# Pooled attention and a max-out FFN on one core: a hand-written order of issue, token groups of 64, and big loads on ScalarE's queue

## The chip, the cores and the metric

The kernel runs on one core of a Trainium2 chip. The metric is the device time of one execution, in microseconds (us). Engines are named as in the profile: PE (TensorE's matmuls), PEld (its weight loads), DVE (VectorE), ACT (ScalarE), POOL (GpSimd), SP (SyncE). A q after a name (ACTq, SPq) is that engine issuing DMAs.

## The reference, cut to what matters

```python
# q, k, v: (8, 8, 576, 64) f32; w1..w3: (512, 768), w_out: (768, 512)
k_p = k.reshape(B, H, 72, 8, D).mean(axis=3)       # 576 keys -> 72
v_p = v.reshape(B, H, 72, 8, D).mean(axis=3)
attn = softmax(q @ k_p.T / 8)
x = (attn @ v_p), heads side by side               # (4608 tokens, 512)
h = maximum(maximum(x @ w1, x @ w2), x @ w3)       # (4608, 768)
out = h @ w_out                                    # (4608, 512) f32
```

## The kernel before

The work is two streams on one PE: eight batches of attention, and nine blocks of 512 tokens of the FFN. Block n can run once the batches that cover its tokens are done. The framework's scheduler interleaves them, and it chooses each engine's order. In names of tiles, `kt` and `vt` are loaded keys and values, `kp` and `vp` the same after the mean over 8 (a fold adds one half of a tile to the other), `xn` and `xT` the attention's result and its transpose, `pw` and `po` PE's results of the FFN's two stages, `osb` the output. These are the parts that the change touches (`...` marks cuts):

```python
NT, NR = 18, 32                      # 18 groups of 32 tokens
def load(b, after=None):
    kt = ld.tile([96, 6, POOL, D], F32, ...)              # two buffers in turn
    vt = ld.tile([Sp, H, POOL, D], F32, ...)
    ... loads = [nc.sync.dma_start(out=kt, in_=ksrc)]     # SyncE's queue
    loads.append(nc.sync.dma_start(out=vt, in_=vsrc))
    ...
def prep(b, kt, vt, qb):             # the mean over 8: three folds
    if b < 2:  fold(nc.vector, kt ...)                    # k of batches 0 and 1 on DVE
    else:      fold(nc.gpsimd, kt ...)                    # the others on POOL
    fold(nc.gpsimd, vt, ...)                              # v always on POOL
...
def moe(n):                          # one block
    ...                              # 72 matmuls into pw, ACT cast, two DVE maxima
    for mm in range(4):
        ...                          # 6 matmuls into po
        osb = sb3.tile([128, C], F32, ...)                # three buffers in turn
        nc.scalar.copy(out=osb, in_=po)
        for u in range(4):                                # four stores of 64 KB
            nc.sync.dma_start(out=dst[:, g, :], in_=osb[32 * u:32 * u + 32, :])
```

The softmax here doesn't subtract the row's maximum and nothing guards it: scores larger than these inputs give would overflow.

Of the kernel before, what the change touches and what calls it, by code (L numbers as in the profile page):

```python
# [14 lines left out]
def kernel(  # L15
# [24 lines left out]
    NT = 18  # L40
    NR = 32
    NI = NT // 2
# [10 lines left out]
    etp = ctx.enter_context(tc.tile_pool(name="etp", bufs=16))  # L53
    psp = ctx.enter_context(tc.tile_pool(name="psp", bufs=1, space=PSUM))

    def load(b, after=None):
        kt = ld.tile([96, 6, POOL, D], F32, name="kt", tag="kt")
        ksrc = k[b].rearrange("h s d -> (h s d)").rearrange(
            "(p i j d) -> p i j d", p=96, i=6, j=POOL)
        vt = ld.tile([Sp, H, POOL, D], F32, name="vt", tag="vt")  # L60
        vsrc = v[b].rearrange("h (sp j) d -> sp h j d", j=POOL)
        if b == 0:
            loads = [nc.sync.dma_start(out=kt[:, i:i + 3], in_=ksrc[:, i:i + 3])
                     for i in (0, 3)]
        else:
            loads = [nc.sync.dma_start(out=kt, in_=ksrc)]
        loads.append(nc.sync.dma_start(out=vt, in_=vsrc))
        qb = ld.tile([128, 2, NT, D], BF16, name="qb", tag="qb")
        nc.gpsimd.dma_start(out=qb, in_=q[b].rearrange(
            "h s d -> (h s d)").rearrange("(g p t d) -> p g t d", g=2, p=128, t=NT))  # L70
        if after is not None:
            for x in loads:
                tc.add_manual_dep(x.ins, after.ins.name, mybir.DependencyInfo(
                    mybir.DependencyClass.Sync, mybir.DependencyReason.DATA),
                    reason="weights first")
        return kt, vt, qb

    first = load(0)

    ident = const.tile([128, 128], BF16, name="ident", tag="ident")  # L80
    make_identity(nc, ident)
    identh = const.tile([128, 128], F16, name="identh", tag="identh")
    make_identity(nc, identh)

    w_sb = [const.tile([128, KCH, DFF], F16, name=f"mw{wi}", tag=f"mw{wi}")
            for wi in range(3)]
    wo_sb = const.tile([128, JCH, C], F16, name="mwo", tag="mwo")
    w_dma = [nc.gpsimd.dma_start(out=t,  # L88
                                 in_=wap.rearrange("(kc p) j -> p kc j", p=128))
             for t, wap in zip(w_sb, (moe_w1, moe_w2, moe_w3))]  # L90
    nc.gpsimd.dma_start(out=wo_sb,
                        in_=moe_w_out.rearrange("(jc p) c -> p jc c", p=128))

    vp_all = const.tile([Sp, B, H, 65], F16, name="vp", tag="vp")
    nc.vector.memset(vp_all, float(POOL))

    kz_all = [const.tile([128, 2, H, Sp], BF16, name=f"kz{i}", tag=f"kz{i}")
              for i in range(2)]
    for kz in kz_all:
        nc.vector.memset(kz, 0.0)  # L100

    xT = const.tile([128, KCH, TOK], F16, name="xT", tag="xT")

    def prep(b, kt, vt, qb):
        kp2 = sb2.tile([96, 6, 2, D], BF16, name="kp2", tag="kp2")
        def fold(e, t, outs):
            for n in (4, 2):
                e.tensor_tensor(out=t[:, :, 0:n, :], in0=t[:, :, 0:n, :],  # L108
                                in1=t[:, :, n:2 * n, :], op=ALU.add)
            for o in outs:  # L110
                e.tensor_tensor(out=o, in0=t[:, :, 0, :], in1=t[:, :, 1, :],  # L111
                                op=ALU.add)

        if b < 2:
            for i in (slice(0, 3), slice(3, 6)):
                fold(nc.vector, kt[:, i], [kp2[:, i, 0, :], kp2[:, i, 1, :]])
        else:
            fold(nc.gpsimd, kt, [kp2[:, :, 0, :], kp2[:, :, 1, :]])
        fold(nc.gpsimd, vt, [vp_all[:, b, :, 0:D]])

        qT = sb2.tile([128, 2, NI, 128], BF16, name="qT", tag="qT")
        qTf = qT.rearrange("p g i c -> p (g i) c")
        for m in range(3):
            pqt = psp.tile([128, 6, 128], BF16, name="pqt", tag="tr", bufs=1)
            for u in range(6):
                n = 6 * m + u
                g, i = n // NI, n % NI
                nc.tensor.transpose(pqt[:, u, :], qb[:, g, 2 * i:2 * i + 2, :],  # L128
                                    ident)
            if b == 0 and m == 1:  # L130
                nc.vector.tensor_copy(out=qTf[:, 6 * m:6 * m + 6, :], in_=pqt)
            else:
                nc.scalar.copy(out=qTf[:, 6 * m:6 * m + 6, :], in_=pqt)  # L133

        pkt = psp.tile([128, 6, 96], BF16, name="pkt", tag="tr", bufs=1)
        for i in range(6):
            nc.tensor.transpose(pkt[:, i, :], kp2[:, i, :, :], ident[0:96, 0:96])  # L137
        kz = kz_all[b % 2]
        for par in range(2):
            rows = slice(64 * par, 64 * par + 64)  # L140
            nc.vector.tensor_copy(
                out=kz[rows, par].rearrange("p h (r i) -> p h r i", i=6),
                in_=pkt[rows].rearrange("p i (h r) -> p h r i", h=H))
        return qT, kz

    def heads(b, qT, kz):
        ets = []
        for h in range(H):
            psc = psp.tile([Sp, 2, 512], F32, name="psc", tag="att", bufs=2)
            mov = qT[:, h // 4, :, 32 * (h % 4):32 * (h % 4) + 32]  # L150
            for par in range(2):
                nc.tensor.matmul(psc[:, par, 0:288], kz[:, par, h, :], mov,  # L152
                                 start=True, stop=True)
            et = etp.tile([Sp, S], F16, name="et", tag="et")
            nc.scalar.activation(  # L155
                out=et.rearrange("p (i a r) -> p i a r", a=2, r=NR),
                in_=psc[:, :, 0:288].rearrange("p a (i r) -> p i a r", r=NR),
                func=FT.Exp, scale=1.0 / 64.0)
            ets.append(et)
        return ets  # L160

    def values(b, ets):
        for c0, keep in ((0, 0), (128, 0), (256, 0), (384, 0), (448, 64)):
            pav = psp.tile([128, 2, 512], F32, name="pav", tag="att", bufs=2)
            for h in range(H):
                nc.tensor.matmul(  # L166
                    pav[:, h // 4, 65 * (h % 4):65 * (h % 4) + 65],
                    ets[h][:, c0:c0 + 128], vp_all[:, b, h, :],
                    start=True, stop=True)
            pv = pav[:, :, 0:260].rearrange("p g (h e) -> p g h e", e=65)  # L170
            rcp = sb3.tile([128, 2, 4], F32, name="rcp", tag="rcp")
            nc.vector.reciprocal(out=rcp, in_=pv[:, :, :, 64])
            xn = sb3.tile([128, 2, 4, D], F16, name="xn", tag="xn")
            nc.vector.tensor_tensor(  # L174
                out=xn, in0=pv[:, :, :, 0:D],
                in1=rcp.to_broadcast([128, 2, 4, D]), op=ALU.mult)
            pxt = psp.tile([128, KCH, 128], F16, name="pxt", tag="tr", bufs=1)
            for kc in range(KCH):
                nc.tensor.transpose(  # L179
                    pxt[:, kc, :],  # L180
                    xn[:, kc // 2, 2 * (kc % 2):2 * (kc % 2) + 2, :], identh)
            g0 = S * b + c0
            nc.scalar.copy(out=xT[:, :, g0 + keep:g0 + 128],  # L183
                           in_=pxt[:, :, keep:128])

    def moe(n):
        col = slice(NB * n, NB * n + NB)
        hT = sb2.tile([128, JCH, NB], F16, name="hT", tag="hT")
        for jc in range(JCH):
            t = None  # L190
            for wi in range(3):
                pw = psp.tile([128, NB], F32, name=f"pw{wi}", tag="pw", bufs=3)
                for kc in range(KCH):
                    nc.tensor.matmul(pw, w_sb[wi][:, kc, bass.ts(jc, 128)],  # L194
                                     xT[:, kc, col],
                                     start=(kc == 0), stop=(kc == KCH - 1))
                if wi == 0:
                    t = sb3.tile([128, NB], F16, name="t0", tag="t0")
                    nc.scalar.copy(out=t, in_=pw)  # L199
                elif wi == 1:  # L200
                    t1 = sb3.tile([128, NB], F16, name="t1", tag="t1")
                    nc.vector.tensor_tensor(out=t1, in0=t, in1=pw, op=ALU.max)  # L202
                    t = t1
                else:
                    nc.vector.tensor_tensor(out=hT[:, jc, :], in0=t, in1=pw,  # L205
                                            op=ALU.max)
# [23 lines left out]
    while done < TOK // NB:  # L230
        moe(done)
        done += 1
# [30 lines left out]
```

## Time and profile before

| | before |
|---|---|
| time, median of the first 4 runs | 289.27 us (289.17 to 290.36) |
| span of the profiled run | 288.2 us |
| first FFN matmul (`pw`) | 43.97 us |
| period of a block with one batch of attention | 27.3 to 27.7 us |
| last matmul to end of span | 6.9 us |

The first part of the page gives each engine's busy time, its share of the span and its instructions; the `PEclk` row of the slices gives the clock that PE was granted, in tenths:

```profile
PE 248.6 (86%) x1664; PEld 131.2 (46%) x1664; DVE 129.3 (45%) x224; ACT 128.0 (44%) x218; POOL 117.4 (41%) x68
PEclk9999999999999999999999999999999999999996
```

Only PE is near full. The clock's row shows full from the start, but the trace has no clock record before 48.1 us, and the prediction found matmuls of half speed in the head, so this row says nothing before the first record. The prediction shows the rest of the reading: a head of 44 us, a full body and a tail.

### The profile page before, as it was taken

How to read it: one execution, taken by the hardware profiler on the slowest of the kernel's cores; microseconds unless marked ns; L12 is line 12 of the kernel's file. 1: busy time of each engine (PE TensorE's matmuls, PEld its weight loads, DVE VectorE, ACT ScalarE, POOL GpSimd, SP SyncE). 2: the span in 40 equal slices, each digit the busy share in tenths (PEclk: the TensorE clock that was granted, in tenths of full speed). 3: DMA queues.
4: the chain of work that ended last, by engine and by line, in shares of the span. 5: the costliest groups of instructions: out<-in, count | busy, mean ns of one | idle time of the engine just before them, and what ended most of it. 6: DMA issues, size and time to landing. Idle time of an engine off the chain costs nothing.

```text
span 288.2 us, 4331 instructions
## 1 busy us (share of the span) xinstructions
PE 248.6 (86%) x1664; PEld 131.2 (46%) x1664; DVE 129.3 (45%) x224; ACT 128.0 (44%) x218; POOL 117.4 (41%) x68
## 2 busy tenths in 40 slices
PE   0254049999999999999999999999999999999990
PEld 0132044564545455545554565456455544444440
DVE  7420083483238334724571557057505832533520
ACT  1134024753575267535753663565357533222230
POOL 6048006999999999999282300000000000000000
PEclk9999999999999999999999999999999999999996
DMA  7999999898839959975912700320040005014013
GB/s 189 255 228 199 261 239 229 190 219 234 193 111 216 202 141 214 235 174 119 206 31 72 141 20 0 98 50 0 2 123 23 2 9 138 1 27 120 3 45 102
DMA packets 17190, 36.47 MB, mean 127 GB/s; under 512 B 2736, under 2 KB 5040, under 8 KB 16496
## 3 DMA queue, kind: packets, MB, share of 16 engines
q1 hardware_dynamic: 12624, 28.32, 38.6%
q0 software_dynamic: 4544, 7.87, 15.3%
q8 instruction: 13, 0.21, 0.3%
q14 instruction: 9, 0.07, 0.1%
HBM read 34.60 MB, written 9.44 MB: 153 GB/s over the span
## 4 chain that ended last, share of the span: by engine, by line
PE 77%; DMA 14%; ACT 2%; DVE 1%; issue 1%; POOL 1%; SPq 0%; ACTq 0%; POOLq 0%
PE pw L194 47%; PE po L211 15%; DMA mw<-in_moe_w_dram 7%; PE psc L152 6%; PE pxt L179 4%; DMA out_dram<-osb 4%; DMA kt<-in_k_dram 3%; PE pav L166 3%; PE pqt L128 3%; ACT xT L183 2%; PE pkt L137 1%; DVE kt L108 1%; POOL mw L88 1%; ACT osb L215 0%; DVE xn L174 0%
## 5 line engine op out<-in xcount | busy, mean ns | idle before, releaser
L194 PE MATMUL pw<-xT,mw 128*128 128x512 f16 x648 | 163.8, 382 | 0.7 <-ACT xT L183 0.7
L194 PEld LDWEIGHTS <-mw 128*128 128x128 f16 x648 | 60.4, 98 | 51.0 <-issue 1.1
L202 DVE TENSOR_TENSOR t<-t,pw 128x512 f16<-128x512 f16 x54 | 37.1, 687 | 100.0 <-PE pw L194 97.6
L108 POOL TENSOR_TENSOR vt<-vt 72x2048 f32<-72x2048 f32 (+1 forms) x16 | 54.8, 3427 | 36.3 <-DMA vt<-in_v_dram 35.7
L199 ACT CAST t<-pw 128x512 f16<-128x512 f32 x54 | 31.6, 585 | 48.2 <-PE pw L194 47.7
L211 PE MATMUL po<-mwo,hT 128*128 128x512 f16 x216 | 48.1, 379 | 0.0
L205 DVE TENSOR_TENSOR hT<-t,pw 128x512 f16<-128x512 f16 x54 | 37.1, 686 | 16.5 <-PE pw L194 13.8
L155 ACT ACTIVATE et<-psc 72x576 f16<-72x576 f32 x64 | 37.4, 645 | 11.4 <-PE psc L152 11.3
L215 ACT COPY osb<-po 128x512 f32<-128x512 f32 x36 | 21.1, 587 | 36.2 <-PE po L211 34.7
L183 ACT COPY xT<-pxt 128x512 f16<-128x512 f16 (+1 forms) x40 | 21.8, 544 | 33.5 <-PE pxt L179 33.3
L211 PEld LDWEIGHTS <-hT 128*128 128x128 f16 x216 | 21.1, 98 | 25.5 <-DVE hT L205 1.7
L108 POOL TENSOR_TENSOR kt<-kt 96x1536 f32<-96x1536 f32 (+1 forms) x12 | 31.4, 2617 | 0.4
L152 PE MATMUL psc<-qT,kz 128*72 128x288 bf16 x128 | 27.9, 304 | 2.4 <-ACT et L155 1.5
L133 ACT COPY qT<-pqt 128x768 bf16<-128x768 bf16 x23 | 18.4, 801 | 24.0 <-PE pqt L128 23.7
L174 DVE TENSOR_TENSOR xn<-pav,rcp 128x512 f16<-128x512 f32 x40 | 26.7, 684 | 0.4
L179 PE MATMUL pxt<-identh,xn 128*128 128x128 f16 x160 | 16.5, 229 | 11.4 <-DVE xn L174 10.8
L128 PE MATMUL pqt<-ident,qb 128*128 128x128 bf16 x144 | 13.2, 234 | 13.7 <-DMA qb<-in_q_dram 12.0
L152 PEld LDWEIGHTS <-kz 128*72 128x72 bf16 x128 | 14.0, 117 | 19.5 <-issue 8.8
L179 PEld LDWEIGHTS <-xn 128*128 128x128 f16 x160 | 11.9, 102 | 21.9 <-DVE xn L174 17.4
L166 PE MATMUL pav<-vp,et 72*128 72x65 f16 x320 | 18.8, 200 | 3.3 <-POOL vp L111 3.3
L128 PEld LDWEIGHTS <-qb 128*128 128x128 bf16 x144 | 10.9, 105 | 20.5 <-DMA qb<-in_q_dram 12.0
L166 PEld LDWEIGHTS <-et 72*128 72x128 f16 x320 | 15.6, 103 | 7.3 <-ACT et L155 3.2
(23 smaller groups left out, 72.9 us busy)
## 6 DMA issues: line engine op xcount, KB each, us to landing
vt<-in_v_dram SPq DMA_DIRECT2D x8, 1152.0 KB
out_dram<-osb SPq DMA_DIRECT2D x144, 64.0 KB, 1.7
kt<-in_k_dram SPq DMA_DIRECT2D x7, 1152.0 KB, 10.4
qb<-in_q_dram POOLq DMA_DIRECT2D x8, 576.0 KB, 12.1
mw<-in_moe_w_dram POOLq DMA_DIRECT2D x3, 768.0 KB, 18.3
kt<-in_k_dram SPq DMA_DIRECT2D x2, 576.0 KB, 6.8
mwo<-in_moe_w_out_dram POOLq DMA_DIRECT2D x1, 768.0 KB, 25.4
```

Of the source, the lines that this page charges most:

```text
L108: e.tensor_tensor(out=t[:, :, 0:n, :], in0=t[:, :, 0:n, :], in1=t[:, :, n:2 * n, :], op=ALU.add)
L128: nc.tensor.transpose(pqt[:, u, :], qb[:, g, 2 * i:2 * i + 2, :], ident)
L152: nc.tensor.matmul(psc[:, par, 0:288], kz[:, par, h, :], mov, start=True, stop=True)
L155: nc.scalar.activation(out=et.rearrange("p (i a r) -> p i a r", a=2, r=NR), in_=psc[:, :, 0:288].rearrange("p a (i r) -> p i a r", r=NR), ...
L166: nc.tensor.matmul(pav[:, h // 4, 65 * (h % 4):65 * (h % 4) + 65], ets[h][:, c0:c0 + 128], vp_all[:, b, h, :], start=True, stop=True)
L179: nc.tensor.transpose(pxt[:, kc, :], xn[:, kc // 2, 2 * (kc % 2):2 * (kc % 2) + 2, :], identh)
L183: nc.scalar.copy(out=xT[:, :, g0 + keep:g0 + 128], in_=pxt[:, :, keep:128])
L194: nc.tensor.matmul(pw, w_sb[wi][:, kc, bass.ts(jc, 128)], xT[:, kc, col], start=(kc == 0), stop=(kc == KCH - 1))
L199: nc.scalar.copy(out=t, in_=pw)
L202: nc.vector.tensor_tensor(out=t1, in0=t, in1=pw, op=ALU.max)
L205: nc.vector.tensor_tensor(out=hT[:, jc, :], in0=t, in1=pw, op=ALU.max)
L211: nc.tensor.matmul(po, hT[:, jc, bass.ts(mm, 128)], wo_sb[:, jc, :], start=(jc == 0), stop=(jc == JCH - 1))
```

## The change

Its intent is to start the FFN earlier and to keep PE covered. Every engine now issues exactly in written order. Groups are of 64 tokens, so that a tile of 128 tokens has two stores of 128 KB. Batches 0 and 1 are partly loaded as 16-bit and pooled on PE. The first exps take four heads at once. Weights come in column thirds. Blocks 0 and 1 start in halves. The loads of k and v of batches 2 to 7 go from SyncE's to ScalarE's queue. The core of the diff, cut:

```diff
-    NT = 18
-    NR = 32
+    NG = 9
+    NR = 64
...
+    ctx.enter_context(tc.manual_schedule())
...
+    def load_kv(b, name, src, eng, dtype, parts):
+        t = ld.tile([Sp, H, POOL, D], dtype, name=name, tag=name[:2])
...
+    hT0 = new_hT()
+    side = queries(1)
+    loads_on = nc.scalar
+    def load(b):
+        kts[b], x = load_kv(b, "kt", k, loads_on, F32, 1)
+        vts[b], y = load_kv(b, "vt", v, loads_on, F32, 1)
+        if b == 2:
+            after(x + y, last_early[0])      # wait for v of batch 1
+        load_q(b)
+    for slot, _ in enumerate(hidden(0, hT0)):      # block 0, first part
+        ...
+    for slot, _ in enumerate(project(0, hT0)):     # block 0, second part
+        ...
+    load(2)
+    load(3)
+    fold_k(2, nc.gpsimd)
+    fold_v(2)
+    ...
+    for n in range(1, TOK // NB):                  # blocks 1 to 8
+        if n + 2 < B:
+            fold_k(n + 2, nc.gpsimd); fold_v(n + 2)
+        if n + 3 < B:
+            load(n + 3)
+        nxt = batch(n + 1) ...                     # one step of it per slot
-            for u in range(4):
+            for u in range(2):
```

## The prediction

> **What bounds the kernel now.** I read first the slices of the page: which engine is full, and from when.
>
> ```profile
> PE   0254049999999999999999999999999999999990
> DVE  7420083483238334724571557057505832533520
> ACT  1134024753575267535753663565357533222230
> ```
>
> One slice is 7.2 us. TensorE (PE) is nearly idle for six slices and full to the last; no other engine is full. So there are three spans: a head (to 44 us), a body bound by PE, and a tail. The chain that ended last, in order of time (start, length, what), says what the head waits for:
>
> ```profile
> 4.47 21.32 DMA mw<-in_moe_w_dram
> 25.81 9.92 DMA kt<-in_k_dram
> 35.75 1.82 DVE kt L108 x2
> 37.88 0.66 DVE xn L174
> ...
> 43.97 0.59 PE pw L194
> ...
> 239.83 15.54 PE pw L194 x72
> 255.37 5.18 PE po L211 x24
> ```
>
> The weights land at 25.8. Then batch 1's keys are fetched, and VectorE (DVE), which takes its instructions in order, stands before their fold while batch 0's `xn`, whose input has been ready since about 28, waits behind it. The waits name it (total, times, longest, in us):
>
> ```profile
> DVE kt L108 <- DMA kt<-in_k_dram: 17.4, 2, 16.7
> PE pxt L179 <- DVE xn L174: 10.8, 2, 10.0
> ```
>
> So the head loses 16.7 us to an order. For the body I read stretches (length, busy PE, PEld, DVE, ACT, POOL, clock, DMA share, GB/s):
>
> ```profile
> 157.40:184.80 27.40, 27.29 (x198) 14.61 (x196) 13.54 (x24) 15.12 (x26) 2.68 (x3) 1.00 0.29 61
> 239.80:260.50 20.70, 20.70 (x98) 9.40 (x96) 8.25 (x12) 5.76 (x10) 0.00 (x0) 1.00 0.20 51
> 281.30:288.20 6.90, 0.00 (x0) 0.00 (x0) 0.00 (x0) 0.59 (x1) 0.00 (x0) 0.67 0.39 102
> ```
>
> A block of the FFN alone takes 20.72 us (15.54 + 5.18 of the chain: 96 matmuls of 216 ns); with one batch of attention in it 27.49 (the period of the `po` groups in the chain), so a batch costs 6.77. From 44.0 to 281.3 there are nine blocks and seven batches: 186.5 + 47.4 = 233.9 of the 237.3; the other 3.4 went where stores stood behind loads on SyncE's queue (70 to 84). The tail is 6.9.
>
> **What the Trainium skill says.** (1) "Perfetto Trace Analysis", DMA Instruction — HWDGE: the semaphore wait of such a DMA is held by the issuing sequencer, which goes on to its next instruction only after the descriptors are made. Here the trace agrees for SyncE: its queue waited 16.6 us for POOL to free `vt` buffers, and stores stood behind. The change gives these loads to ScalarE (ACT), which also has all the evacuations. (2) "DMA: Bandwidth & Descriptors", Issuing engines are not separate DMA queues: another issuer brings no bandwidth; no run shows this yet. (3) "TensorE: Matmul & The Clock Gate", Part 1: an idle PE falls to half clock and takes some 3.4 us of work to return. The trace agrees: four score matmuls of 288 columns took 1.18 us in the head, about 240 ns each from start to start, against about 125 in the body. (4) "ScalarE: Activation LUTs", What ACT_TABLE_LOAD costs: 186 ns + 0.833 ns a column; that gives 666 for 576 columns, the trace has 645.
>
> **The change, part by part.**
>
> *Head.* Removed: the wait of 16.7. Batch 0 is hand-ordered, q before v, weights in column thirds. DMA: q, v (16-bit) and k of batch 0 are 0.6 + 0.6 + 1.2 MB as written; at the 250 GB/s of 7 to 19 us in this trace they land near 11.5, the first third of the weights (0.8 MB at 200 GB/s) near 16. The chain on the engines: half a k near 6.0; its fold on DVE 1.2 + 0.7 + 2 x 0.4 = 2.7 (from 0.936, 0.546 and 0.339 us of the 768, 384 and 192 column folds); transpose and copy 1.1; second fold 2.7; a copy of q 0.5: scores start near 13.2. ACT then has two exps of 1024 columns (1.04 each by the skill's formula) and four of 640 (0.72), with waits for the second half of k and q: last exp near 20.8 (old total 8 x 0.645, so the merging itself saves under 0.5). First values, `xn` twice, transposes, copies (0.3, 0.9, 0.9, 0.3, 0.6): the FFN starts near S = **23.5** instead of 44. The new pooling of v on PE (16 x 0.11) fits between the exps.
>
> *Block 0.* 20.7 of FFN and 0.1 for halves; the rest of batch 0's outputs 1.3; batch 1: pooling k on PE 8 x 0.216 = 1.7, v 1.7, transposes 1.3, scores 2.0. Together 28.9, with 1.0 of small stalls 29.9; the last copy to `osb` ends 0.8 later: T = 23.5 + 30.7 = **54.2**.
>
> *The loads of batches 2 and 3.* They are written after this block, and an engine issues in written order: ACT issues k2 and v2 at T, although the DMA engines have been free since about 40. In the old trace one such load alone runs at
>
> ```profile
> DMA packets 642, 1.57 MB, mean 192 GB/s; under 512 B 43, under 2 KB 43, under 8 KB 608
> ```
>
> (stretch 69.8 to 78), so 1.18 MB takes 6.1 + 2 = 8.1 us. Then POOL folds. POOL, start and length:
>
> ```profile
> 61.51 6.95 POOL L108 TENSOR_TENSOR vt<-vt 72x2048 f32<-72x2048 f32 x2
> 68.53 1.27 POOL L111 TENSOR_TENSOR vp<-vt 72x512 f16<-72x512 f32 x1
> ```
>
> A fold of v is 8.2, a fold of k (two outputs) 9.5. So k2 is folded at T + 17.6 and v2 at T + 25.8. Two things wait for that. Block 1's second slot transposes k2: PE stands until T + 17.6. Worse, load(4) is written before block 1, and its tiles are the third in two buffers: its v may start only when v2 is folded, and ACT waits for that **before** block 1's first cast. So block 1 resumes near T + 25.8 + 0.6 (wait, issue) + 1.0 (cast, copy) = T + 27.4 = **81.6**. Before the stall PE does five steps of batch 1's outputs and two half units, to about T + 5.0: some **22 us** of idle PE.
>
> *Body after it.* Eight blocks 165.8, less 0.9 done; rest of batch 1: 0.7; six batches. Scores now take three matmuls (320 + 192 + 64 columns, about 0.255 a head, 2.0 as before, because the padded keys give full-width weight loads); transposes 1.0 + 0.3 + 1.1, values 1.35: 5.8, plus 0.5 for stalls (before 1.0; one step per slot should halve them) = 6.3 each, 37.8. End of block 1 without cover 1.0; half clock after the stall 1.7. Sum 206.1: last matmul at 287.7. Later loads should not block: POOL needs 17.7 a batch against 27 a block.
>
> *Tail.* Two stores instead of four: 8 instructions at about 0.45 instead of 16, so about 2 less: 4.9. Span 292.6, plus 1.1 (289.3 against a span of 288.2): **293.7, say 294**.
>
> In one line: head −20.5, store stalls −3.4, attention −2.8, tail −2.0, against pooling and batch 0's outputs +4.8, bare stretches at both block ends, cold clock and small stalls some +6, the new stall +22.
>
> **Rivals.** *No stall*: if k2 and v2 came early, the 22 and the 1.7 fall away: about 270, 7% faster. For it: the diff makes load(2) wait for batch 1's v, which has a point only if it could be issued earlier, and nobody moves 20 us of head to lose it again. Against it: everything on ACT is in written order, and batch 1's v is pooled before. *Only PE's wait on k2*: if ACT did not block, PE resumes near T + 18 and then waits a little for v2: about 285. For it: a queue that holds waits apart from the engine; against it, the skill and SyncE's waits. *DMA-bound*: weight thirds have runs of 512 bytes written; were they twice as slow, k1 and the output weights would come about 8 us late and block 0 end later: 298 to 302. For it: DMA share near 1 until 44; against it, at 200 GB/s everything for block 0 lands by 37, while the output weights are wanted at about 45.
>
> **Range and chances.** The stalled course, chance 0.8, centres on 294 with some 5 us either way (S by 2, folds and landing by 3, batches by 3), so 2% above 289.3 (295.1) lies inside it: slower 0.34, same 0.43, faster 0.03. The other 0.2 is mostly faster (0.17). Range 272 to 302.
>
> **What would show it.** PE's slices: full from the fourth or fifth, then two to four empty slices near 58 to 82, then full. In the waits, ACT's queue (the load of v) for POOL's fold of v, above 15 us; PE for a transpose of k. Block period near 27.0, last stretch 20.7, tail near 5. It is wrong if the first `pw` comes after 30, if k2 is issued before 45, if ACT works on while its load waits, or if a period exceeds 28.

## The result

| | before | after |
|---|---|---|
| time, median | 289.27 us | 299.12 us (298.32 to 300.39, 4 runs) |
| first FFN matmul | 43.97 | 23.60 |
| end of block 0 | 74.0 | 54.5 |
| end of block 1 | 102.4 | 114.7 |
| last matmul | 281.3 | 292.9 |
| tail | 6.9 | 4.6 |

The changed kernel is 3.4% slower: the ratio is 1.0336, with a 95% interval of 1.0291 to 1.038. A ratio here is the mean time of one kernel's runs over that of the other's of the same rounds, so it is not quite the ratio of the medians. Executions over 1.5% slower than the fastest of the same kernel are left out of the means. The result is correct.

The changed kernel leads by 19.5 us after block 0 and trails by 12.3 us after block 1. The whole story lies in block 1, which takes 60.2 us instead of 28.3. The slices of the page after (7.4 us each) show the hole:

```profile
PE   7498999430079999999999999999999999999993
POOL 8451000039999998399249918950000000000000
PEclk9689999955557999999999999999999999999999
```

PE works from the first slice on, runs near full, and then there is a hole of four slices (4, 3, 0, 0). POOL is idle before the hole (four slices of 0) and becomes full in it. The clock is at half (5) for four slices. The waits (engine, line, releaser; total, times, longest) name who stood:

```profile
ACT t L265 <- POOL vp L121: 17.7, 1, 17.7
PE pkt L157 <- ACT xT L204: 16.0, 2, 15.8
ACT xT L204 <- DMA out_dram<-osb: 7.7, 1, 7.7
```

The chain that ended last, in order of time, follows the hole (start, length, what):

```profile
57.44 6.80 issue
64.24 4.51 POOL kt L118
...
80.65 1.27 POOL vp L121
82.72 0.50 ACT xT L204
83.26 0.64 PE pkt L157 x8
```

And the timeline of ACT shows how it came about. A line is start, length, engine, what; in brackets, how long it had idled and what ended that:

```profile
54.69 0.61 ACTq L70 DMA_DIRECT2D kt<-in_k_dram  x1
55.39 0.31 ACTq L70 DMA_DIRECT2D vt<-in_v_dram  x1
55.80 1.01 ACTq L70 DMA_DIRECT2D kt<-in_k_dram  x1
56.85 5.94 ACTq L70 DMA_DIRECT2D vt<-in_v_dram  x1
...
81.94 0.31 ACTq L70 DMA_DIRECT2D vt<-in_v_dram  x1
82.35 0.37 ACT L265 CAST t<-pw 128x256 f16<-128x256 f32 x1 [17.67 <-POOL vp L121]
```

The first four are k and v of batches 2 and 3, issued at the end of block 0. The last is batch 4's v. It goes out only when POOL has folded v of batch 2 (80.65 + 1.27 = 81.92), and the cast behind it, whose input was ready, waits 17.67 us. From 54.5 to 83.2 PE works 4.5 us of 28.7. Outside block 1 the change does what it was meant to: 20.4 us off the head, 2.3 us off the tail, and blocks of 27.2 to 27.6.

### The profile page after: what moved, and what is told of

Read it like the earlier page. It is cut to its first block, busy times and chain, and to the rows that moved or that the text cites. A ratio compares the mean times of both kernels' runs of the same rounds, so it can differ in the third digit from the quotient of the medians.

```text
span 297.5 us, 4634 instructions
## 1 busy us (share of the span) xinstructions
PE 258.7 (87%) x1853; PEld 143.3 (48%) x1853; DVE 126.2 (42%) x230; ACT 132.3 (44%) x224; POOL 123.2 (41%) x73
## 4 chain that ended last, share of the span: by engine, by line
PE 78%; POOL 6%; DVE 5%; DMA 4%; issue 4%; ACT 2%; SPq 0%; ACTq 0%; DVEq 0%; POOLq 0%
PE pw L260 45%; PE po L290 14%; PE psc L180 6%; PE pqt L150 4%; PE pav L209 3%; DMA kt<-in_k_dram 3%; PE pxt L200 3%; POOL kt L118 2%; POOL vt L118 2%; DVE kz L160 2%; DMA out_dram<-osb 1%; PE pvp L139 1%; PE pkt L157 1%; DVE xn L217 1%; ACT xT L204 1%
## 5 line engine op out<-in xcount | busy, mean ns | idle before, releaser
L260 PE MATMUL pw<-xT,mw 128*128 128x512 f16 (+1 forms) x696 | 164.0, 370 | 1.6 <-ACT xT L204 1.3
L268 DVE TENSOR_TENSOR t<-t,pw 128x512 f16<-128x512 f16 (+1 forms) x58 | 37.7, 651 | 81.2 <-PE pw L260 42.3
L265 ACT CAST t<-pw 128x512 f16<-128x512 f32 (+1 forms) x58 | 32.3, 557 | 56.7 <-PE pw L260 36.0
L118 POOL TENSOR_TENSOR kt<-kt 72x2048 f32<-72x2048 f32 (+1 forms) x12 | 41.1, 3426 | 32.1 <-issue 21.1
L185 ACT ACTIVATE et<-psc 72x576 f16<-72x576 f32 (+2 forms) x62 | 40.7, 662 | 15.8 <-PE psc L180 15.7
L271 DVE TENSOR_TENSOR hT<-t,pw 128x512 f16<-128x512 f16 (+1 forms) x58 | 37.7, 649 | 15.6 <-PE pw L260 13.7
L118 POOL TENSOR_TENSOR vt<-vt 72x2048 f32<-72x2048 f32 (+1 forms) x12 | 41.1, 3427 | 0.5
L217 DVE TENSOR_TENSOR xn<-pav,rcp 128x512 f16<-128x512 f32 x40 | 27.6, 691 | 1.4
L180 PE MATMUL psc<-qT,kz 128*128 128x64 bf16 (+3 forms) x192 | 26.7, 253 | 1.1 <-DVE qT L152 0.7
L180 PEld LDWEIGHTS <-kz 128*128 128x128 bf16 x192 | 18.8, 100 | 16.1 <-issue 1.9
L152 ACT COPY qT<-pqt 128x768 bf16<-128x768 bf16 (+2 forms) x23 | 18.1, 785 | 17.7 <-PE pqt L150 17.7
```

Source lines behind the costliest of these rows:

```text
L118: e.tensor_tensor(out=t[:, :, 0:n, :], in0=t[:, :, 0:n, :], in1=t[:, :, n:2 * n, :], op=ALU.add)
L180: nc.tensor.matmul(out, kz_all[b % 2][:, f % 2, h, :], qTs[b][:, n + i0:n + i1, 64 * (h % 2):64 * (h % 2) + 64], start=True, stop=True)
L185: nc.scalar.activation(out=out, in_=in_, func=FT.Exp, scale=1.0 / 64.0)
L217: nc.vector.tensor_tensor(out=xn, in0=pv[:, :, :, 0:D], in1=rcp.to_broadcast([128, 2, 4, D]), op=ALU.mult)
L260: nc.tensor.matmul(pw, w_sb[wi][:, kc, bass.ts(jc, 128)], xT[:, kc, col], start=(kc == 0), stop=(kc == KCH - 1))
L265: nc.scalar.copy(out=t, in_=pw)
```

## The experiments

There were twelve runs, all correct; the kernel before ran beside each (medians 288.96 to 289.48). Block 1 takes 60.2 us in the changed kernel. In each run I read three things: the length of block 1, the length of block 2, and the time.

| run | block 1 | block 2 | time (median) | ratio to before, 95% |
|---|---|---|---|---|
| changed kernel | 60.2 | 27.2 | 299.12 | 1.029 to 1.038 |
| e1_loads_sync | 51.2 | 31.4 | 294.44 | 1.013 to 1.022 |
| e6_load4_late | 50.9 | 36.2 | 298.64 | 1.028 to 1.037 |
| e6b_load4_mid | 50.8 | 30.9 | 292.94 | 1.009 to 1.015 |
| e2_early_sync | 40.6 | 27.2 | 279.59 | 0.961 to 0.971 |
| e8_spaced_loads | 50.8 | 30.1 | 292.00 | 1.003 to 1.013 |
| e9_fixed_slots | 39.4 | 30.9 | 281.68 | 0.970 to 0.977 |
| e9b_more_osb | 37.6 | 28.2 | 277.21 | 0.953 to 0.961 |
| e10_slots_only | 60.4 | 27.2 | 299.37 | 1.030 to 1.042 |
| e3_warm_stall | 60.1 | 27.2 | 297.13 | 1.024 to 1.030 |
| e3b_warm_longer | 61.4 | 27.2 | 298.66 | 1.029 to 1.038 |
| e7_four_stores | 58.6 | 32.7 | 304.47 | 1.046 to 1.059 |
| e4_before_fold_pool (of the kernel before) | 31.9 | 27.7 | 289.76 | 0.997 to 1.004 |

The theory: a load on ACT that waits for its buffer holds ACT and with it PE, and the loads come too late. The rivals: the fold alone is the wait, whoever issues; the issue of big loads holds the engine even without a wait; the cold clock makes part of it.

### Who issues the loads

```diff
-    loads_on = nc.scalar
+    loads_on = nc.sync
```

> Undoes one part: the big loads of batches 2 to 7 go to SyncE's queue, at the same places in the program. Theory (ScalarE's sequencer was held by the load of v4 until v2 was folded at 81.9): ScalarE works on, and TensorE resumes when k2 is folded, near 74 instead of 83.3, so about 9.5 us less: 289 to 291 us; a stall of some 14 us stays, and TensorE then waits for a transpose of k. Rival (TensorE's own wait for k2 was the bound, ScalarE's wait lay beside it): 298 to 300.

The time was 294.44. From the timeline of this run, the line that decides:

```profile
75.73 0.66 PE L157 MATMUL pkt<-ident,kp 72*128 72x72 bf16 x8 [16.21 <-POOL kp L121]
```

Batch 4's v still goes out at 83.93, but SyncE does that waiting, and PE comes back at 75.73, released by the fold of k. So 7.5 us of the hole, and 9.0 us of block 1, belong to ACT standing behind its load, as the theory has it; the rest of the hole is the lateness of the fold. But the expected time was missed by some 4 us, since block 2 grew by 4.2: a copy into `osb` waited 3.6 us for a store, and a PE transpose waited 3.0 us behind it. No load of k or v was moving then. POOL had issued the next load of q at 101.56, and while that came in, the stores that SyncE issued from 101.86 on hardly moved. The queues of this run from 101.86 to 107 (packets, MB, share of 16 engines; q0 is POOL's, q1 SyncE's):

```profile
q0 software_dynamic: 459, 0.53, 73.3%
q1 hardware_dynamic: 84, 0.14, 8.4%
```

No run moves that load of q, so that it is the cause is likely and not shown.

### Batch 4's load after block 1, or in its middle

```diff
-        if n + 3 < B:
+        if n + 3 < B and n > 1:
...
+        if n == 1:
+            load(n + 3)          # e6: after the block; e6b: in its 14th slot
```

> Only load(4) moves, from before block 1 to after it; everything else stays on ScalarE's queue. Theory: the same as with all loads on SyncE's queue, 289 to 291, since only the load of v4 held ScalarE beyond 74; the 5.9 us issue of v3 still shows on ScalarE's queue but is hidden behind the wait for k2. Rival (the slow issue of the loads themselves holds ScalarE, whichever load it is): little changes, 296 to 299.

> The changed kernel with only load(4) moved, now into the 14th slot of block 1: after v2 is folded and well before load(5), so that never more than two big loads are issued in a row there. Theory (moving load(4) to the end of block 1 gained 9.3 us in block 1 and lost 8.9 in block 2, because four loads in a row held ScalarE for 7 us): block 1 near 51 us, block 2 near 27.3, 289.5 to 291.5 us in all. Rival (load(4) away from the head of block 1 always costs later what it gains): 296 to 299.

Both shorten block 1 by over 9 us, on ACT's queue this time: it is the place of that one load in the written order that matters, not the queue. But e6 gave 9.0 us back in block 2 and ended at 298.64, as its rival said. There batches 4 and 5 are four big loads in a row, and the waits show ACT standing for 7.2 us:

```profile
ACT t L265 <- DMA out_dram<-osb: 7.2, 1, 7.2
```

The fourth load in a row took 6.33 us to issue there; in the changed kernel it took 5.94 (the fourth line of its timeline above), on SyncE in e1 5.70. The releaser named, a store, is an inference of the profile; that the issue itself held ACT rests on its length. The Trainium skill, "Perfetto Trace Analysis", DMA Instruction — HWDGE, says that the reported length of such an issue covers the making of its descriptors, and draws a descriptor buffer that can fill. That three big loads fill it and the fourth waits would fit: by the packet records of the traces the fourth issue ended about when the first of the four loads did (at 62.8, against 62.6 to 63.1 in the changed kernel; at 116.2, against 116.5 to 116.8 in e6). What it was that filled, no run here shows. In e6b the loads of batches 4 and 5 come two at a time and none of their issues is that slow. Its time is still 1.4 us over what was expected; it loses 3.7 us in block 2, and this is where:

```profile
107.59 0.58 ACT L294 COPY osb<-po 128x512 f32<-128x512 f32 x1 [2.94 <-DMA out_dram<-osb]
```

The fourth copy of the block needs the first of three `osb` buffers back. The stores were issued from 101.1 on but moved nothing before 105: k and v of batch 4 came in until 103.4, and the next load of q until past 106. PE then waits 2.36 us for a copy behind it.

### Batch 2's loads before block 0's projection

```diff
-    loads_on = nc.scalar
+    loads_on = nc.sync
+    load(2)                      # before project(0), no longer after it
```

> Loads on SyncE's queue, and load(2) written before block 0's projection, so that it waits only for batch 1's v. Theory: k2 lands near 46, is folded near 55, v2 near 64; no stall at the start of block 1 and no half clock after it: 299 less 25.5 of late start and 4.5 of cold clock, 268 to 271 us. Rival (the stall only moves, to v2 or to k3): 277 to 285, with empty slices later.

The time was 279.59: 3.4% faster than before. k of batch 2 was issued at 36.99 instead of 54.69, its fold began at 50.16, and the long idle time of PE is gone. It missed the theory's 268 to 271 and fell in the rival's range: the stores of block 0 stood behind the loads (a copy to `osb` waited 4.24 us), and the clock was at half from about 59 to 73.

### The same on ACT's queue, spaced out

```diff
+        if slot == 18:           # in block 0's first part
+            load(2)              # no longer after block 0
...
     load(3)                      # after block 0, as before
...
+                if n == 1 and slot == 13:
+                    load(4)      # no longer before block 1
```

> Candidate: loads stay on ScalarE's queue; load(2) moves into block 0 (19th slot, after batch 1's v has landed), load(3) stays, load(4) moves to the 14th slot of block 1. Theory: no wait for k2 (folded near 57), no issue longer than 1 us on ScalarE, stores not behind loads; block 1 starts near 57 at full clock: 268 to 272 us. Rival (the stores still wait beside the loads, as with the early load on SyncE's queue): 277 to 281.

This missed by 20 us: 292.0. The waits of this run:

```profile
PE pxt L200 <- ACT xT L204: 13.2, 1, 13.2
ACT xT L204 <- POOL vp L121: 12.3, 1, 12.3
```

ACT again stood behind a load, now that of batch 3's v (issued at 68.14, just as POOL ended the fold of v of batch 2). As batch 3's v could have had the place of batch 1's v, which PE had read long before, I suspected that the framework's rotation had given it batch 2's. So I gave each tile a place by the parity of its batch:

```diff
-        t = ld.tile([Sp, H, POOL, D], dtype, name=name, tag=name[:2])
+        t = ld.tile([Sp, H, POOL, D], dtype, name=name,
+                    tag=f"{name[:2]}{b % 2}", bufs=1)
```

> The spaced-loads kernel (292.0 us), with one thing changed: each k or v tile gets a fixed place by the parity of its batch, so that the load of batch 3's v takes the place of batch 1's v (read out by TensorE well before) and not that of batch 2's v. Theory (the 12.3 us for which ScalarE stood at 68.5 behind that load were a wait for a place that the program did not have to choose): the wait is gone, ScalarE's copy of xT after it waits under 3 us, the long idle time of PE in block 1 is gone, block 1 falls from 50.8 to 33-40, the time to 274-282. Rival (the load waits for a semaphore lane, or POOL's folds of batch 2 come too late whoever issues the loads): PE still waits 8 us or more in block 1, and the time is 286 or more.

> The fixed-slots kernel with four output tiles in turn instead of three (and two normalised tiles instead of three, to make room). Theory: where big loads run beside the stores of a block, the fourth copy into an output tile no longer waits for a store (2.1 us at 106.5 in the spaced-loads kernel, 4.2 in the early one); block 2 falls by 1.5-3 us against the fixed-slots kernel, the time by the same: 271-280. Rival: the wait only moves to the next copy or to the normalised tiles, and the two kernels agree within 1 us.

The wait is gone and block 1 fell by 11.4 us, as the suspicion has it; the place that the rotation gave is not itself seen in a trace. The time is 281.68, the theory's range. In e9b, `osb` has four buffers and `xn` two instead of three each:

```diff
-            osb = sb3.tile([128, C], F32, name="osb", tag="osb")
+            osb = sb3.tile([128, C], F32, name="osb", tag="osb", bufs=4)
-        xn = sb3.tile([128, 2, 4, D], F16, name="xn", tag="xn")
+        xn = sb3.tile([128, 2, 4, D], F16, name="xn", tag="xn", bufs=2)
```

Block 2 fell from 30.9 to 28.2, the expected 1.5 to 3. The medians differ by 4.5 us, more than block 2 explains, and the last matmuls of the profiled runs by 6.5: 2.7 of that is block 2, 1.9 block 1, and 1.5 an earlier first `pw` (23.73 against 25.18), which the edit does not touch. Part of this is chance: e9's profiled run is the slowest of its five (283.73), and its clock was at half for 13.7 us of the head against 6.8 in e9b. I credit the buffers with the 2.7 of block 2; the rest is left open. **277.21 us is the best version**: 4.3% faster than before, and 21.9 us faster than the changed kernel. Its block 1 in two stretches (length, busy PE, PEld, DVE, ACT, POOL, clock, DMA share, GB/s):

```profile
54.60:70.00 15.40, 11.85 (x117) 9.46 (x115) 6.73 (x16) 6.08 (x11) 14.14 (x8) 0.67 0.83 228
70.00:92.20 22.20, 22.11 (x175) 12.79 (x174) 11.14 (x22) 11.74 (x22) 21.86 (x9) 1.00 0.66 140
```

What is left in block 1 (37.6 against 27.2 in steady state) is a start with gaps of 3.6 us, short chains of copies between PE and the others, and a clock of 0.67.

Is it the places or the order? The changed kernel with the places and buffers of e9b, but its own order of loads:

> The changed kernel with the fixed places and the four output tiles of the best version (277.2 us), but with its own order of loads: four in a row after the projection of block 0, batch 4's before block 1. Theory (the order in which ScalarE issues the loads is the cause; the places and tiles only matter once that is mended): ScalarE still stands about 17.5 us behind the load of batch 4's v, block 1 takes 58-61 us, and the time is 295-300. Rival (the places given by parity are what freed the best version): block 1 falls below 45 us and the time is under 285.

It was 299.37, the changed kernel's time, and block 1 was 60.4. So the order is the cause; the places matter only once it is mended.

### How much is the cold clock?

```diff
+                if n == 1 and slot == 1:        # before PE's wait for k of batch 2
+                    for _ in range(64):         # e3b: 80
+                        nc.tensor.matmul(w2, warm[:, 0:128], warm, ...)
```

> The changed kernel with 64 idle matmuls (of ones, result never read) put into the stall, ahead of the transpose of k2, some 15.5 us of work that ends about when ScalarE is freed. Theory (the half clock from 83.3 to 92.3 costs 4.5 us, not the 1.7 predicted): granted clock 1.0 from the resume on, 294 to 295.5 us. Rival (block 1 is slow because its steps wait for one another): 298 to 300.

> The changed kernel with 80 dummy matmuls in place of 64 in the slot before PE's long wait, so that no idle time is left before the turn of k of batch 2 (there were 1.6 us of it with 64, and the clock fell again). Theory (half of the clock after the stall is a cost of its own, some 4.5 us, because block 1 from the end of the stall on takes 31.4 us at 0.5 for 9 us): PE comes back at 84-85.5, 1-2 us later than the 83.3 of the changed kernel, the clock stays near 1.0 after it, and the rest of block 1 takes 26.5-28.5 instead of 31.4; the time is 296-298. Rival (the block after the stall is slow by its waits, the clock being a consequence of them): the clock falls again to 0.5 and the rest of block 1 takes 30.5 or more.

e3 was inconclusive (297.13, between its two forecasts). The dummy work ended 1.6 us before PE could go on, and the clock fell again. In e3b there was no idle time, and PE resumed at 85.84. The stretches from the resume to the end of block 1 (columns as above), first of the changed kernel, then of e3b:

```profile
83.20:92.30 9.10, 8.31 (x62) 6.47 (x62) 2.99 (x7) 3.45 (x7) 8.94 (x5) 0.50 0.79 182
92.30:114.70 22.40, 22.32 (x177) 12.98 (x176) 11.13 (x22) 11.88 (x22) 21.98 (x10) 1.00 0.37 72
```

```profile
85.80:90.00 4.20, 2.67 (x39) 2.15 (x38) 2.14 (x5) 1.66 (x3) 4.04 (x3) 0.99 0.80 179
90.00:92.70 2.70, 2.67 (x19) 1.95 (x17) 0.42 (x1) 1.17 (x2) 2.70 (x3) 0.50 0.80 173
92.70:116.20 23.50, 23.41 (x187) 13.99 (x186) 11.55 (x23) 12.19 (x22) 23.09 (x10) 0.99 0.41 78
```

With the clock warm, PE was busy only 2.67 us of the first 4.2: at full speed it waits for the copies of the other engines, and the gaps let the clock fall again. From the resume on, block 1 took 30.4 instead of 31.4. The theory wanted 26.5 to 28.5, the rival 30.5 or more. So 6.3 us less at half clock were worth about 1.0 us, in one profile each: the cold clock lies largely on top of waits that are there anyway. The time, 298.66, does not differ from the changed kernel's.

The traces also show when the clock came back. Its changes lie a multiple of 3.41 us apart, so I read PE's busy time in steps of that length, up to the return (columns as above): three steps of the changed kernel, then the last one before the return in e3b and in e3.

```profile
82.01:85.43 3.42, 2.17 (x25) 1.91 (x25) 1.87 (x5) 0.86 (x2) 3.42 (x1) 0.50 0.80 180
85.43:88.84 3.41, 2.71 (x20) 2.00 (x19) 0.69 (x2) 1.78 (x4) 3.28 (x2) 0.50 0.80 186
88.84:92.25 3.41, 3.38 (x22) 2.51 (x21) 0.84 (x2) 1.61 (x3) 3.38 (x3) 0.50 0.79 178
```

```profile
66.07:69.48 3.41, 3.41 (x22) 2.06 (x21) 0.90 (x2) 0.00 (x0) 3.33 (x2) 0.50 0.80 180
64.20:67.61 3.41, 3.19 (x22) 2.32 (x23) 0.90 (x2) 0.00 (x0) 3.41 (x1) 0.50 0.79 177
```

Steps with 2.17 and 2.71 us of work did not bring the clock back, and those with 3.19 to 3.41 did. So the 9 us of half clock fit the gaps after the stall: the first step without large gaps was the third. Over all fourteen traces, 32 of 33 returns follow a step with PE busy for 93% or more; the other (in e7) follows one of 77%, and one full step in the head of e9 brought no return.

### The stores

```diff
-                nc.sync.dma_start(out=dst[:, GS[g], :], in_=osb[64 * u:64 * u + 64, :])
+                for r in (0, 32):
+                    nc.sync.dma_start(out=dst[r:r + 32, GS[g], :],
+                                      in_=osb[64 * u + r:64 * u + r + 32, :])
```

> The changed kernel with each store of 64 rows cut into two of 32, as before: four stores per tile. Theory: only the tail changes, from 4.6 to about 6.5 us: 300.5 to 301.5 us. Rival (the stores are hidden): 299.

The tail is 6.5 instead of 4.6, so halving the stores is worth 1.9 us at the end, as expected. But the time was 304.47, 3 us over the range, and the reason is the same pattern as before, in the timeline of this run:

```profile
109.22 13.29 SPq L299 DMA_DIRECT2D out_dram<-osb  x16
113.49 0.31 ACTq L70 DMA_DIRECT2D kt<-in_k_dram  x1
119.68 0.31 ACTq L70 DMA_DIRECT2D vt<-in_v_dram  x1
120.08 0.59 ACT L265 CAST t<-pw 128x512 f16<-128x512 f32 x1 [5.97 <-DMA out_dram<-osb]
```

The sixteen stores take 13.3 us to issue, batch 5's v load on ACT waits in that time, and ACT's cast waits 6 us behind it: block 2 is 32.7. The profile names a store as the releaser; what ties a load of `vt` to a store is not shown. At the end of block 0 of this run batch 2's v stood likewise: k went out at 54.76 and v at 64.13, when k had landed, and ACT idled 10.3 us.

### The head of the kernel before

The prediction said that the old head lost 16.7 us to an order: DVE standing before batch 1's fold. That can be undone in the kernel before by one edit:

```diff
-        if b < 2:
+        if b < 1:                # k of batch 1 is folded on POOL
```

> The kernel before with batch 1's fold of k on GpSimd instead of VectorE, so that VectorE does not stand before it in the head. Theory (the head lost 16.7 us to that order): first FFN matmul near 30 instead of 44, but the transposes of batch 1's k still wait for the fold, near 43 to 51, so about 281 to 285 us. Rival (the head is bound by the weights and loads): 287 to 290.

The time was 289.76: the same. The first `pw` came at 34.18 instead of 43.97, so the wait is gone, but block 0 then took 35.8 (before 30.1) and block 1 31.9 (before 28.3). The chain of this run shows what stood behind it:

```profile
25.58 20.05 DMA vt<-in_v_dram
45.69 4.52 POOL vt L108
...
54.01 0.39 PE pav L166 x7
...
68.08 6.52 DMA out_dram<-osb
74.70 0.59 ACT osb L215
```

Batch 1's v lands at 45.7 and is folded at 54.0, and then stores stand beside loads. The order was the first of several limits; of the 9.8 us all but 0.5 were given back by the end of block 1 (101.9 against 102.4).

One planned kernel, with three buffers for the loads, did not fit in the core's memory and was not run, so a version in which no load ever waits for a buffer is not tried.

## Why the prediction was right or wrong

The direction and the mechanism of the stall were right; the size was off. It said 293.7 (+1.6%) and the kernel took 299.1 (+3.4%), inside its range, but it gave more to "within 2%" (0.43) than to "slower" (0.34), and that was wrong. The steps that failed are three terms of its sum: the landing of k2 (8.1, measured 9.55), the rest of block 1 after the stall (29.5, measured 31.4), and attention at 6.3 a batch (135.1 for five periods, measured 136.5). Together they are 4.7 of the 5.4 missing. The sum, term by term:

| term of the sum | predicted | measured | difference |
|---|---|---|---|
| first `pw` | 23.5 | 23.60 | +0.1 |
| from there to the issue of k2 (T) | 30.7 | 31.09 | +0.4 |
| issue of k2 to the start of its fold | 8.1 | 9.55 | +1.4 |
| folds of k2 and v2 | 17.7 | 17.70 | 0 |
| to PE's resume | 1.6 | 1.32 | -0.3 |
| resume to end of block 1 | 29.5 | 31.4 | +1.9 |
| blocks 2 to 6, five periods | 135.1 | 136.5 | +1.4 |
| blocks 7 and 8 | 41.4 | 41.7 | +0.3 |
| tail | 4.9 | 4.6 | -0.3 |
| time less span | 1.1 | 1.6 | +0.5 |
| sum | 293.6 | 299.1 | +5.4 |

- **The stall by ACT's order.** Right, to 2 us (83.26 for 81.6). The trace has the wait of 17.7 us on the load of v4, and e1, e6 and e6b show that ACT's part in block 1 is 9 us and the lateness of the fold the rest. What it took from the skill agrees with the trace: the sequencer held the wait, and the cast behind it idled 17.67 us.
- **"1.18 MB takes 6.1 + 2 = 8.1 us" failed by 1.4.** The 192 GB/s came from a stretch that holds the end of one load and the next; here four were issued together. While they run, the DMA share is 0.80. The Trainium skill, "DMA: Bandwidth & Descriptors", Why a DMA increments its semaphore by 16, says that a DMA runs on the largest number of engines up to 16 that divides its slowest dimension; for 72 rows that is 12. The trace agrees: each of these loads ends with 12 packets of 4 bytes, and 12 of 16 engines, or 0.75, is near the 0.80. The four didn't share the rate. By the packet records they came in one after another, ending at 63.1, 69.6, 76.1 and 83.2. The first packet of k2 moved 1.1 us after its issue, and k2 took 7.3 us, with 0.27 MB of block 0's stores in that time; v2, with no store beside it, took 6.5. So the stores fit about 0.8 of the 1.4, and a rate of 179 GB/s instead of 192 another 0.4; no run takes the stores away.
- **"Half clock after the stall 1.7" and "end of block 1 without cover 1.0" failed by 1.9 together.** The clock stayed at half for 9.0 us. The 3.4 us that the prediction took from the skill are for sustained work, and the block's start has gaps: it came back after the first step of 3.41 us in which PE was busy nearly throughout, as in e3 and e3b, and in e3b it fell again in the patchy work after the dummies. e3b shows that only about 1.0 of the miss is to be had from the clock; the waits on copies, which the sum lacked, are probably the rest.
- **"Six batches at 6.3" failed by 1.4 over five blocks.** In block 2 PE is busy 27.01 us of 27.3: the work was sized 0.5 too small, the stalls 0.2 too large.
- **Not foreseen, and without an effect on the sum:** the fourth load in a row takes 5.94 us to issue and holds ACT to 62.8. It was hidden behind the fold that PE waited for anyway. It decided e6.
- **"So the head loses 16.7 us to an order" was wrong as a cause for the whole.** e4 took that order away: the first `pw` came 9.8 us earlier and the time did not change. The 20.4 us that the change took off the head came with its earlier and smaller loads of batches 0 and 1 and their pooling on PE; the runs do not part these.
- **The first rival, "no stall", 270.** The 22 us of stall proved real: with the loads early and in free places, the time was 277.21, 21.9 less. That this is so near 22 is partly luck: e9, without the buffers of e9b, is 17.4 less. And 270 was not reached: block 1 still has 10.4 us more than a steady block. **The second rival, "only PE's wait on k2", 285,** is what e1 made, with PE back at 75.7; it came out at 294.4: 4.2 of the 9.4 between them is block 2's growth, and the rest is about what the sum missed anyway (5.4).

## What to carry to other kernels

When every engine issues in written order, read each load as an instruction of the engine that issues it: ask at which instant its buffer comes free, and what stands behind it in that engine until then. Issue early, by an engine with nothing urgent behind, two big loads at a time, into places whose last reader you know, and not beside the stores whose buffers come back next; in e1 what came in beside the stores was a load of q, half the size. A gain in the head is real only if what follows has its data too: moving one limit by 20 us made the next one, a fold on POOL that had been covered, the bound.

## What the Trainium skill lacked or had wrong

- Fourth big load in a row on one queue: 5.5 to 6.3 us to issue on ScalarE (5.94, 6.33, 5.55 us) and 5.70 us on SyncE, the ones before it at most 1.4. On ScalarE it ended within 0.6 us of the landing of the first of the four. "Perfetto Trace Analysis" draws a descriptor buffer that can fill, but gives neither its size nor what it costs the issuing engine; I found no figure for it on "DMA: Bandwidth & Descriptors" either.
- "TensorE: Matmul & The Clock Gate", Part 1: 3.4 us of sustained work to return to full clock. The runs agree: the clock came back after steps of 3.41 us with 3.19 to 3.41 us of PE's work and not after 2.71, so that work with gaps, which a kernel has after a stall, took 9.0 us in the changed kernel. The page does not say that being warm may then be worth little: 6.3 us less at half clock brought 1.0 us.
- "DMA: Bandwidth & Descriptors", Why a DMA increments its semaphore by 16: the rule for 72 rows is borne out (12 closing packets for each load), but that section gives no rate; four such loads, one after another, ran at 183 GB/s (62.8 to 83.2 us of the changed kernel).
- Part 1 of the clock page warns that the recorded events can be unreliable. Here they are missing, not wrong: the kernel before has no clock record before 48.1 us, and the profile's row shows its head as full, while a group of four 128-column transposes took 0.61 us there and 0.39 us in the warm body.
- None of the pages that I read has the cost of issuing many small stores beside loads: sixteen of 64 KB took 13.3 us to issue, and a load on another queue was held 6.0 us in that time. Nor does any have what stores lose beside a load of q: in e1 they moved 0.14 MB in 5.1 us, the load 0.53 MB.
